# A one-token attention and feed-forward kernel: other load order, the feed-forward moved to the middle, and the output gathered in eight adjacent partitions

## The chip, the cores and the metric

The kernel runs on one core of one Trainium2 chip. A core has TensorE (PE, matrix products; its weight loads are shown as PEld), VectorE (DVE), ScalarE (ACT), GpSimd (POOL) and SyncE (SP), which run their own instruction lists and meet at semaphores, and 16 DMA engines that carry out the transfers which SP and ACT issue. The metric is the device time of one execution in microseconds (us); lower is better.

## The reference, cut to what matters

Two tokens (batch B = 2, one position each, D = 448) go through a layer norm; the result `xn` feeds an attention over the last W = 2048 positions of a given cache, and a small feed-forward net that gates it:

```
xn = layernorm(x)                                   # 2 x 448
q  = (xn @ wq)            -> 16 heads of 256        # wq 448 x 4096
k, v = caches[:, :, -2048:, :], 8 kv heads, each used by 2 query heads
p  = softmax(q . k / 16)                            # over 2048 positions
s  = (p @ v, all heads side by side) @ wo           # wo 4096 x 448
h  = relu(xn @ w1)                                  # w1 448 x 1792
g  = silu(h @ w2)                                   # w2 1792 x 448
out = x + s * g
```

All tensors are bfloat16. The arithmetic is tiny; the bytes are not. K and V are 4 x 4096 KB each, wq and wo 3584 KB each, w1 and w2 1568 KB each: 44.1 MB in all, each byte read once.

## The kernel before

**Units.** The work is cut into four units u = 0..3 (`NU`): batch u // 2, and four of the eight kv heads. The 128 partitions hold the 4 heads x 32 runs of positions; a partition holds 64 positions (`NT`) of one head. For a unit, `do_T` (16 calls, one for each chunk of four positions per partition) transposes K on PE into one of five PSUM banks `tb0`..`tb4`, and DVE or ACT evacuates it to `kt`; `do_S` multiplies four transposed chunks by the queries (`qz`) into the bank `sbk`; `softmax` finds the maximum (DVE, with two short PE steps to bring it across partitions), shifts, exponentiates on ACT, transposes the weights on PE and sums; `do_PV` multiplies them by V, in four quarters of eight products each; `attend_scale` divides by the sum (DVE) and `attend_turn` brings the result to the layout `at_exp`. `scores(u)` is all chunks of `do_T` with the `do_S` between them.

**Order.** Every engine's list is the order in which the Python code records its operations; there is no scheduler. On PE: the sixteen transposes of unit 0, the query projection `do_q` (L390), the scores and softmax of unit 0, then for u = 1, 2, 3 `scores(u)` and `softmax(u, values(u-1))`, where the PV products of the unit before fill the gaps in the softmax. After unit 3's softmax come, on PE, the feed-forward net (`do_H`, `do_hT`, `do_F`, L413 to L443), then `do_PV(3)`, its scale and turn, two products that spread `at_exp` into `at2` (one a batch, L500), and the output projection (L506 to L511).

**Column groups.** Products with few output rows are issued in fours with `tile_position=(0, 32*i)`: each writes its own 32 of the 128 PSUM partitions, so four run at once in four column groups of the array. The output projection has 32 steps j of four products with 112 columns each; the weights have two columns (the two batches). Its result therefore stands in partitions 0, 1, 32, 33, 64, 65, 96, 97. `do_F` is made in the same way with 14 steps.

**Loads.** SP issues all large loads, in the order in which they are recorded, and each waits for its buffer: K0, wq, K1 and V0 at once; K2 after the transposes of unit 0 (L202), V1 after the query product, K3 after the transposes of unit 1, V2 after PV of unit 0; w1 and w2 (into `kbuf0`, L478) after the transposes of unit 2; V3 in two parts after PV of unit 1; wo (into `kbuf1`, L488) in five parts of 12, 12, 4, 2 and 2 steps after the transposes of unit 3. wq lies in `vbuf1` until V1 takes its place.

**End.** DVE multiplies by the gate and adds x (L513, L515); SP and ACT each store one batch (L517), four partitions that lie 32 apart, and SP waits for both stores (L519).

## Time and profile before

| | us |
|---|---|
| median of 4 runs (112.70 to 112.95) | 112.85 |
| the profiled execution | 112.70 |
| its span, first to last instruction | 110.9 |
| outside the span | 1.8 |
| PE busy / weight loads | 74.9 (68%) / 50.1 (45%) |
| DVE busy | 48.1 (43%) |
| ACT busy | 35.3 (32%) |
| SP's DMA queue, share of 16 engines | 93.5%, 44.11 MB |

Times in the profile are counted from the start of the span. The profile has a page (busy times, the span in 40 slices, the queues, the chain that ended last, the costliest groups) and views that are asked for: the chain of waits in order of time, the timeline of a window (start, length, engine, line, operation, output <- inputs, count, and in brackets the idle time before it with what ended it), stretches with busy time and granted clock, and the durations at one source line. "128*4 128x512" in a row is 128 rows by 4 weight columns, and a moving operand of 128 partitions by 512.

### The profile page before, as it was taken

The numbers are of one execution on the slowest core, as the hardware profiler recorded it, in microseconds if no ns is written. First come the engines' busy times: TensorE is split into PE (matmuls) and PEld (weight loads), VectorE is DVE, ScalarE is ACT, GpSimd is POOL, SyncE is SP. The second block draws the span as 40 slices with busy tenths as digits, with TensorE's granted clock in tenths as the row PEclk, the third lists the DMA queues.
The fourth block names the chain that finished last, engine by engine and source line by source line (L and its number), as shares of the span: only waits on it lengthen the run. The fifth ranks groups of instructions, "written<-read, shape, count | busy, mean of one in ns | idle before, by whom it ended". The sixth has DMA issues, their size and how long they took to land.

```text
span 110.9 us, 1921 instructions
## 1 busy us (share of the span) xinstructions
PE 74.9 (68%) x845; PEld 50.1 (45%) x845; DVE 48.1 (43%) x110; ACT 35.3 (32%) x43; POOL 2.0 (2%) x11
## 2 busy tenths in 40 slices
PE   0010299995338999859999949699985667293480
PEld 0000299952027977413777513297632336022350
DVE  2182042953534256553776653477546231404001
ACT  1960036760020647602276602076820200000000
POOL 6000000000000000000000000000000000000000
PEclk9999999999995589995999995899999755555555
DMA  3988979898899899889989998998999998999920
GB/s 107 461 379 379 520 331 496 355 567 372 378 520 425 378 414 520 384 378 532 417 366 437 479 402 378 520 425 378 401 396 421 502 425 375 398 431 419 400 81 1
DMA packets 2619, 44.22 MB, mean 399 GB/s; under 512 B 306, under 2 KB 564, under 8 KB 948
## 3 DMA queue, kind: packets, MB, share of 16 engines
q1 hardware_dynamic: 2584, 44.11, 93.5%
q8 instruction: 6, 0.10, 0.4%
q10 hardware_dynamic: 28, 0.00, 0.0%
q14 instruction: 1, 0.01, 0.0%
HBM read 44.11 MB, written 0.00 MB: 398 GB/s over the span
## 4 chain that ended last, share of the span: by engine, by line
DMA 56%; PE 34%; DVE 4%; SPq 1%; issue 1%; ACT 1%
DMA kbuf<-in_A_k_cache_dram 34%; PE tb L285 25%; DMA kbuf<-in_A_wo_dram 22%; PE sbk L265 5%; PE obk L265 2%; SPq L36 1%; PE mbk L265 1%; DVE s_sb L335 1%; ACT e_sb L340 1%; DVE rm L318 1%; DVE q_n L399 1%; PE mbk L345 1%; DVE pt L350 0%; DVE qz L409 0%; PE mbk L403 0%
## 5 line engine op out<-in xcount | busy, mean ns | idle before, releaser
L285 PE MATMUL tb<-ident_f,kbuf 128*128 128x128 f32 x256 | 36.5, 306 | 6.4 <-DMA kbuf<-in_A_k_cache_dram 6.4
L285 PEld LDWEIGHTS tb<-ident_f,kbuf 128*128 128x128 f32 x256 | 33.4, 161 | 10.6 <-DMA kbuf<-in_A_k_cache_dram 6.6
L295 ACT ACTIVATE kt<-tb 128x1024 bf16<-128x1024 bf16 x28 | 27.4, 1023 | 26.2 <-PE tb L285 26.2
L293 DVE COPY kt<-tb 128x1024 bf16<-128x1024 bf16 x36 | 24.8, 691 | 21.7 <-PE tb L285 21.7
L265 PE MATMUL obk<-vbuf,pt 128*16 128x512 bf16 x128 | 13.7, 538 | 2.4 <-DMA vbuf<-in_A_v_cache_dram 2.4
L265 PE MATMUL sbk<-kt,qz 128*32 128x512 bf16 x128 | 11.0, 393 | 1.6 <-DVE kt L293 1.1
L340 ACT ACTIVATE e_sb<-s_sb 128x512 bf16<-128x512 f32 x4 | 2.5, 629 | 22.9 <-DVE s_sb L335 22.9
L265 PEld LDWEIGHTS obk<-vbuf,pt 128*16 128x16 bf16 x128 | 3.2, 101 | 7.1 <-DMA vbuf<-in_A_v_cache_dram 3.3
L265 PE MATMUL mbk<-ident,xg 2*128 2x2 bf16 x7 | 0.3, 163 | 7.4 <-DVE xg L237 7.4
L265 PEld LDWEIGHTS sbk<-kt,qz 128*32 128x32 bf16 x128 | 2.7, 94 | 5.4 <-DVE kt L293 2.1
L265 PE MATMUL obk<-kbuf,at 128*2 128x112 bf16 x128 | 3.7, 291 | 2.1 <-DMA kbuf<-in_A_wo_dram 1.8
L372 DVE TENSOR_SCALAR o_sb<-obk,rs 128x512 bf16<-128x512 f32 x4 | 2.9, 737 | 4.3 <-PE obk L265 4.3
L318 DVE TENSOR_REDUCE rm<-sbk 128x4 f32<-128x512 f32 x4 | 2.8, 692 | 4.3 <-PE sbk L265 4.3
L350 DVE COPY pt<-mbk 128x512 bf16<-128x512 bf16 x4 | 1.7, 425 | 5.6 <-PE mbk L345 5.6
L345 PE MATMUL mbk<-ident,e_sb 128*128 128x128 bf16 x16 | 2.2, 286 | 2.6 <-ACT e_sb L340 2.6
L265 PEld LDWEIGHTS obk<-kbuf,at 128*2 128x2 bf16 x128 | 2.6, 112 | 3.1 <-DMA kbuf<-in_A_wo_dram 2.6
L265 PEld LDWEIGHTS mbk<-ident,xg 2*128 2x128 bf16 x7 | 0.3, 100 | 7.4 <-DVE xg L237 7.4
L345 PEld LDWEIGHTS mbk<-ident,e_sb 128*128 128x128 bf16 x16 | 1.3, 122 | 5.0 <-ACT e_sb L340 5.0
L323 PE MATMUL mbk<-ident_f,rm 128*1 128x128 f32 x4 | 1.1, 270 | 3.4 <-DVE rm L321 3.4
L265 PE MATMUL mbk<-one_f,mall 1*128 1x1 f32 x8 | 1.6, 270 | 2.5 <-DVE mall L330 2.5
L335 DVE SCALAR_TENSOR_TENSOR s_sb<-sbk,bias,low 128x512 f32<-128x512 f32 x4 | 3.0, 751 | 0.1
L265 PEld LDWEIGHTS mbk<-ssum,gsum 128*128 128x128 f32 x8 | 1.6, 252 | 3.1 <-DVE pt L350 3.1
(68 smaller groups left out, 37.1 us busy)
## 6 DMA issues: line engine op xcount, KB each, us to landing
kbuf<-in_A_k_cache_dram SPq DMA_DIRECT2D x4, 4096.0 KB, 27.2
vbuf<-in_A_v_cache_dram SPq DMA_DIRECT2D x3, 4096.0 KB, 37.1
vbuf<-in_A_wq_dram SPq DMA_DIRECT2D x1, 3584.0 KB, 20.1
kbuf<-in_B_w_dram SPq DMA_DIRECT2D x2, 1568.0 KB, 23.8
vbuf<-in_A_v_cache_dram SPq DMA_DIRECT2D x1, 3072.0 KB, 25.9
kbuf<-in_A_wo_dram SPq DMA_DIRECT2D x2, 1344.0 KB, 22.2
vbuf<-in_A_v_cache_dram SPq DMA_DIRECT2D x1, 1024.0 KB, 27.8
kbuf<-in_A_wo_dram SPq DMA_DIRECT2D x1, 448.0 KB, 24.3
```

Of the source, the lines that this page charges most:

```text
L36: o = _Op(eng, lambda e: e.dma_start(dst, src), [d for d in deps if d is not None], True)
L265: return lambda e: e.matmul(out_ap, lhsT=lhsT, rhs=rhs, start=start, stop=stop, skip_group_check=True, **kw)
L285: o = pr.op(PE, lambda e, n=n, lo=lo: e.matmul(bank_f[:, n * 128:(n + 1) * 128], lhsT=src_f[:, lo:lo + 128], rhs=ident_f[:, :], start=True ...
L293: evac[n_th] = pr.op(DVE, lambda e: e.tensor_copy(dst[:, :], bank[:, :]), deps)
L295: evac[n_th] = pr.op(ACTE, lambda e: e.activation(dst[:, :], bank[:, :], ACT.Copy), deps)
L318: v = pr.op(DVE, lambda e: e.tensor_reduce(out=rm4[:, :], in_=view(sbk, 0, [[1, 4], [4, 128]]), axis=AX.X, op=ALU.max), [st["S", u]])
L335: v = st["shift", u] = pr.op(DVE, lambda e: e.scalar_tensor_tensor(out=view(s_sb, 0, [[4, 128], [1, 4]]), in0=view(sbk, 0, [[4, 128], [1, ...
L340: a = st["exp", u] = pr.op(ACTE, lambda e: e.activation(e_sb[:, :], s_sb[:, :], ACT.Exp, accum_out=ssum[:, 0:1]), [v, st.get(("Pt", u - 1) ...
L345: o = pr.op(PE, lambda e, j=j: e.matmul(mb16[:, 512 + 128 * j:640 + 128 * j], lhsT=e_sb[:, 128 * j:128 * j + 128], rhs=ident[:, :], start= ...
L350: v = st["pt", u] = pr.op(DVE, lambda e: e.tensor_copy(view(pt[u % 2], 0, [[256, 2], [16, 16], [8, 2], [1, 8]]), view(mb16, 512, [[256, 2] ...
L372: st["osb", u] = st["obk"] = pr.op(DVE, lambda e: e.tensor_scalar(out=o_sb[:, :], in0=obk[:, :], scalar1=rs[:, u:u + 1], scalar2=None, op0 ...
L399: v = st["obk"] = pr.op(DVE, lambda e: e.tensor_scalar(out=q_n[:, :], in0=obk[:, :], scalar1=SCALE, scalar2=None, op0=ALU.mult), [o])
```

## The change

1. **Load order.** SP first loads two of the seven slots of wq (8 KB a partition), then K0, then the other five slots; w1 and w2 are issued behind V0, without a wait, into a buffer of their own (`wf`), so that they come before K2. wo goes into `kbuf0`, which is free after the transposes of unit 2, in six parts of 8, 8, 6, 4, 4, 2 steps; the first 16 steps are the first head group, the other 16 the second.
2. **Feed-forward in the middle.** `do_H`, `do_hT` and `do_F` stand between unit 1's softmax and unit 2's scores on every engine, using the banks `tb0` and `tb1` there.
3. **Eight adjacent partitions.** The weights of `do_F` and of the output projection lie in zeroed buffers with gaps (`h_z`, `at_z`, `GAP` = 11 columns a step); a window of eight columns that starts at 3 - i puts the two batches in rows i and 4 + i. The four products of a step now accumulate into the same eight PSUM rows, without `tile_position`. The gate, the last two DVE operations and x have 8 partitions instead of 128 (or 8 scattered ones), and ACT stores the whole output in one transfer and waits for it.
4. **Spreading per unit.** `attend_turn` writes 128 columns, and a new `attend_spread(u)` (one product, one DVE copy) is done for each unit: for units 0 and 1 in the next-but-one unit's scores, for 2 within PV of unit 3, for 3 ahead of the output projection.
5. **Unit 3.** Its PV goes to another bank (`tb3`, which ACT zeroes after the last evacuation); PE gets products whose result nobody reads, `idle_work`: 3 before PV of unit 3, 3 after `attend_scale(3)`, 1 before the last spread.
6. **Small things.** `low` is laid out over 512 columns, so that the shift (L335) reads and writes plain rows; `qmask` has 8 columns; `fold16` is new; two more buffers are zeroed on POOL.

```diff
-    WO_PARTS = [12, 12, 4, 2, 2]
+    WO_PARTS = [8, 8, 6, 4, 4, 2]
+    NWO = 16
+    FIRST = 2
+    NROW = 4 * B
+    GAP = NROW + 3
...
-        wq_sb, w1_sb, w2_sb, wo_sb = vbuf[1], kbuf[0], kbuf[0], kbuf[1]
+        wq_sb, w1_sb, w2_sb, wo_sb = vbuf[1], wf, wf, kbuf[0]
-        wo_src = A_wo.rearrange("(p j) n -> p (j n)", j=32)
+        wo_src = A_wo.rearrange("(v p j) n -> v p (j n)", v=2, j=NWO)
...
+        d_wq = [pr.dma(SP, wq_sb[:, 0:FIRST * HC], wq_src[:, 0:FIRST * HC])]
         load_k(0)
-        d_wq = pr.dma(SP, wq_sb[:, 0:SLOTS * HC], wq_src)
+        d_wq.append(pr.dma(SP, wq_sb[:, FIRST * HC:SLOTS * HC], wq_src[:, FIRST * HC:SLOTS * HC]))
         load_k(1)
         load_v(0)
+        st["w1"] = pr.dma(SP, w1_sb[:, 0:W2_AT], w1_src)
+        st["w2"] = pr.dma(SP, w2_sb[:, W2_AT:W2_AT + 14 * D].rearrange("p (hf f) -> p hf f", hf=2), w2_src)
...
-                out=view(s_sb, 0, [[4, 128], [1, 4]]), in0=view(sbk, 0, [[4, 128], [1, 4]]), scalar=bias[:, 0:1],
-                in1=view(low, 0, [[0, 128], [1, 4]]), op0=ALU.add, op1=ALU.min),
+                out=s_sb[:, :], in0=sbk[:, :], scalar=bias[:, 0:1], in1=low[:, :], op0=ALU.add, op1=ALU.min),
...
+        def attend_spread(u):
+            b, v = divmod(u, 2)
+            o = st["m_at", u] = pr.op(PE, mm(mbk_ap(256, NWO), at_exp[:, :], fold16[:, :], True, True),
+                                      [st["at", u], v_fold16, st["mbk"]])
+            st["at_z", v] = st["mbk"] = pr.op(DVE, lambda e: e.tensor_copy(
+                view(at_z, NWO * GAP * v + 3 + 4 * b, [[GAP, NWO]]), mbk_ap(256, NWO)), [o, p_z])
...
-                    o = pr.op(PE, mm(view(fbk, 0, [[1, NCOL]], n=B, p0=32 * i), h_sb[:, 2 * f:2 * f + 2], w2_sb[:, lo:lo + NCOL],
-                                     f == 0, f == 13, tile_position=(0, 32 * i)), deps)
+                    o = pr.op(PE, mm(view(fbk, 0, [[1, NCOL]], n=NROW), h_z[:, f * GAP + 3 - i:f * GAP + 3 - i + NROW],
+                                     w2_sb[:, lo:lo + NCOL], f == 0 and i == 0, f == 13 and i == 3), deps)
...
+        def idle_work(n):
+            wbk = tb[2][:, :].bitcast(F32).tensor
+            deps = [evac[NU * NCHUNK - 2], v_fold]
+            for _ in range(n):
+                pr.op(PE, mm(view(wbk, 0, [[1, 512]]), ident[:, :], kt[0][:, 0:512], True, True), deps)
+                deps = []
...
         softmax(1, values(0))
         attend_scale(0)
+        do_H()
+        do_hT()
+        do_F()
         load_v(2)
         scores(2)
...
         load_v(3, (0, 48, 64))
+        d_wo, j0 = {}, 0
+        for n in WO_PARTS:
+            v, j = divmod(j0, NWO)
+            d_wo[j0] = pr.dma(SP, wo_sb[:, j0 * D:(j0 + n) * D], wo_src[v, :, j * D:(j + n) * D], [st["T", 2]])
+            j0 += n
         scores(3)
...
         softmax(3, values(2))
         attend_scale(2)
-        do_H()
-        attend_turn(2)
-        do_hT()
-        do_F()
-        do_PV(3)
+        idle_work(3)
+        do_PV(3, (0,))
+        attend_turn(2)
+        do_PV(3, (1,))
+        attend_spread(2)
+        do_PV(3, (2, 3))
         attend_scale(3)
+        idle_work(3)
         attend_turn(3)
...
+        idle_work(1)
+        attend_spread(3)
...
-                m_o = pr.op(PE, mm(obk[32 * i:32 * i + B, 0:NCOL], at2[:, 2 * j:2 * j + 2], wo_sb[:, lo:lo + NCOL],
-                                   j == 0, j == 31, tile_position=(0, 32 * i)), deps)
+                m_o = pr.op(PE, mm(obk[0:NROW, 0:NCOL], at_z[:, j * GAP + 3 - i:j * GAP + 3 - i + NROW],
+                                   wo_sb[:, lo:lo + NCOL], j == 0 and i == 0, j == 2 * NWO - 1 and i == 3), deps)
...
-        d_o = [pr.dma((SP, ACTE)[b], out[b, 0, :].rearrange("(i n) -> i n", i=4),
-                      view(out_sb, 0, [[1, NCOL]], n=4, p0=b, pstep=32), [v_o]) for b in range(B)]
-        pr.op(SP, None, d_o)
+        d_o = pr.dma(ACTE, out[:, 0, :].rearrange("b (i n) -> (b i) n", i=4), out_sb[:, :], [v_o])
+        pr.op(ACTE, None, [d_o])
```

## The prediction

> **What bounds the kernel now.** I read the queue shares and the slices of the page first, then the chain of waits, then the timeline of the stretches that the change touches, then the granted clock by stretch. The page:

> ```profile
> DMA  3988979898899899889989998998999998999920
> GB/s 107 461 379 379 520 331 496 355 567 372 378 520 425 378 414 520 384 378 532 417 366 437 479 402 378 520 425 378 401 396 421 502 425 375 398 431 419 400 81 1
> q1 hardware_dynamic: 2584, 44.11, 93.5%
> ```

> SP's queue is never empty from slice 2 on. The bytes set the end, in whatever order they come. The chain says the same: two long waits for transfers, and a short tail after the last one.

> ```profile
> 0.74 12.35 DMA kbuf<-in_A_k_cache_dram
> 13.13 10.10 PE tb L285 x64
> ...
> 46.25 25.41 DMA kbuf<-in_A_k_cache_dram
> 71.70 1.97 PE tb L285 x16
> ...
> 83.03 24.44 DMA kbuf<-in_A_wo_dram
> 107.52 0.39 PE obk L265 x8
> 107.92 0.28 DVE tmp L513
> 108.23 0.28 DVE out_sb L515
> ```

> K0 has landed at 13.09, K3 at 71.66, the last piece of wo at 107.47. From K3 to the end of wo 15.27 MB follow (V2, w1, w2, V3, wo) in 35.81 us: 0.426 MB/us, the rate I use. How much room PE has below that is in the timeline:

> ```profile
> 71.70 1.97 PE L285 MATMUL tb<-ident_f,kbuf 128*128 128x128 f32 x16 [1.06 <-DMA kbuf<-in_A_k_cache_dram]
> ...
> 92.46 1.47 PE L265 MATMUL tb<-kbuf,h_sb 128*2 128x112 bf16 x56 [0.39 <-DVE h_sb L432]
> ...
> 96.35 3.59 PE L265 MATMUL obk<-vbuf,pt 128*16 128x512 bf16 x32 [2.41 <-DMA vbuf<-in_A_v_cache_dram]
> ...
> 102.38 1.29 PE L265 MATMUL obk<-kbuf,at 128*2 128x112 bf16 x48 [0.29 <-DVE at L502]
> 105.30 2.02 PE L265 MATMUL obk<-kbuf,at 128*2 128x112 bf16 x72 [1.62 <-DMA kbuf<-in_A_wo_dram]
> ```

> PE waits 1.06 us for K3, 2.41 for V3, 1.62 for wo: little slack in a chain of work from 13 to 96 that is otherwise PE's own. Last, the clock:

> ```profile
> 46.41:49.82 3.41, 1.67 (x18) 0.51 (x16) 2.05 (x6) 0.00 (x0) 0.00 (x0) 1.00 1.05 447
> 49.82:53.24 3.42, 3.42 (x30) 1.15 (x30) 1.33 (x3) 0.72 (x2) 0.00 (x0) 0.50 1.07 460
> 53.64:63.10 9.46, 9.46 (x96) 7.46 (x95) 6.34 (x11) 6.79 (x7) 0.00 (x0) 1.00 1.03 441
> 101.02:104.43 3.41, 1.75 (x52) 1.24 (x50) 0.62 (x3) 0.00 (x0) 0.00 (x0) 0.50 0.98 408
> ```

> Columns: stretch, length, busy PE, PEld, DVE, ACT, POOL, then granted clock, DMA share, GB/s. A stretch half idle (1.67 busy) is followed by one at 0.50; a full one (3.42) by full clock. The output projection ran at 0.50 throughout.

> **The change, part by part.**

> *Loads.* Bytes are the same, so the last piece of wo still lands near 107.5; two more cuts add a little (I take +0.1; 0 to +0.3). Within the queue two things move. The 1.05 MB of wq ahead of K0 delay K0 by 1.05/0.426 = 2.46, to 15.55 (the same-sized last part of V3 follows its first part by 98.81 - 96.34 = 2.47 where PE waits for them). The 3.21 MB of w1 and w2 now precede K2, V1, K3 and V2: 7.5 us later each, K3 at 79.2 and K2 near 59.5 (two units of 4.19 MB before K3). V3 (98.8) and wo keep their places. SP issues seven loads at the start instead of four, 0.6 us each, ahead of use. It issues wo behind V3, which waits for PV of unit 1 (80 in my sum); V2 feeds the engines until 88.9. No gap, nothing.

> *PE until unit 1 is done.* K0 is what PE waits for, so +2.46 passes through T(0), q, unit 0's softmax, T(1), unit 1's softmax. V0 and K1 land where they did (41 and 33, estimates from the rate) and stay hidden. PE reaches 53.78 + 2.46 = 56.24. What T(0) gains or loses by when full clock comes is +-1.

> *Feed-forward in the middle.* Before, T(2) started at 53.64, while DVE still scaled unit 0 (53.90 for 0.73). Now `do_H` waits for that scale: 0.85. From H to the start of F took 89.56 to 92.46 = 2.90 at clock 0.50; its two PE pieces (1.48, 0.54) halve at full clock, so 1.9 to 2.9, I take 2.6. F: 56 products, before in fours, 1.47 us. Without column groups they run one after another. Price at 0.50: the projection's first 48 took 1.29 with one lasting 0.29, so 11 further groups take 1.00, 91 ns for one stream of 112 columns. At full clock: half, 46; the four 128-column transposes of q start (0.40 - 0.22)/3 = 60 ns apart, 52 for 112 columns. I take 50. F is 2.8 (full) to 5.1 (half), taken 3.4. Together 6.85 (5.6 to 8.9). T(2) starts near 63.0 against 53.64. K2 is there. Hidden before: H, F and the gate stood in PE's wait for V3, and DVE and ACT were idle.

> *Units 2 and 3.* T(2) and its softmax took 53.64 to 70.64. The gate chain (0.27 + 0.22 + 0.85 + 0.28 and three hops) now holds `tb1` and stands ahead of DVE's first evacuation: about +0.4; the spread +0.1. T(3) starts at 80.5; K3 (79.2) is no longer what it waits for. T(3) and softmax took 71.70 to 88.56 = 16.86, +0.1: 97.5. The plain `low` may take some hundredths off each shift (0.75); I take nothing.

> *PV of unit 3.* 32 products: 16 took 1.04 at full clock, so 1.9 to 3.4; idle work 0.65 to 1.3; turn 0.27, spread 0.21. 3.0 to 5.2, taken 3.6: 101.1, against 99.94. V3 (98.8) is hidden. Then scale 0.75, turn 0.27, mask 0.23, one spread 0.21 and copy 0.20, five hops: 1.95, where the second spread and copy (0.5) are saved. The three idle products lie under the scale at full clock (0.65 of 0.75) and stick out by 0.5 at half. The projection starts at 103.0 against 102.38.

> *Output projection.* 128 products in a row: 6.4 at full clock, 11.6 at half. Before: 32 groups x 91 = 2.9, mostly waiting for wo. The first 16 steps are in by 103.1 and the rest by 107.5, so from 103.0 on PE is the later one; I take 6.9 (some of it at half clock) and 0.2 for the last to come out: 110.1, against 107.87. [...]

> *End.* From the last product to the end of the span 3.04 now. One store for two: the completion records have ACT's at 110.15 and SP's at 110.51. I take -0.3 (0 to -0.6, both stores left at once). Two DVE operations of 112 columns keep their 0.28.

> **Sum.** 110.1 + 3.04 - 0.3 = 112.85 for the span, against 110.9: +1.95 on the profiled execution of 112.70. That one lies 0.15 below the median, so 112.85 + 1.95 = **114.8**.

> [...]

> **The rivals.**

> *The transfers still set the end (21 in 100).* Idle work keeps full clock and PE catches up, so that T(3) waits for K3. For it: K3 at 79.2 is only 1.3 before my PE. Then: 79.2 + 17.0 = 96.2; the last quarter of PV waits for V3 and ends at 99.5; the projection starts at 101.4, has done 16 steps at 104.6 and all at 108.1 with the last piece at 107.6. Span 108.1 + 3.04 - 0.3 = 110.85: -0.05, time 112.8. It turns faster by 0.23 us (0.2%, what a measurement of this kernel can tell from no change) only if the store saves its full 0.36 and the last piece isn't late. Against: each of the three PE terms must come out at its lower end.

> *Half clock in the tail (12 in 100).* A softmax gap halves the clock, as it did at 87, and the short waits for DVE after PV keep any stretch from being full. PV costs 1.6 more, the projection 1 to 4.7 more: 117.5 to 121. For it: clock 0.50 from 87 to the end now, with 2.56 of 3.42 busy. Against: six to nine us of unbroken products.

> *A gap in the queue (2 in 100).* If PV of unit 1 came after 88.9, V3 and wo would wait; PE would have to lose 9 us more. Each us then costs one.

> **How the numbers follow.** The forecast (113.3 to 116.8 for itself, from the bounds of F, of PV and of the store) has 65 in 100. Its low end already is slower than before by 0.4%. The transfer-bound rival splits into 12 within 0.2% and 9 faster. Slower: 65 + 12 + 2 = 79. The range 112.7 to 117.6 leaves out the deep half-clock end and the best store, about 15 in 100.

> **What would show it.** T(0) starts near 15.5; T(2) near 63 and T(3) near 80 with no wait for K; F's 56 products last about 3 us; wo pieces land before PE asks, so no row of the projection waits for DMA; its products start some 50 ns apart; one store. Wrong, if the projection waits for wo (rival one), if its products are 90 ns apart (rival two), or if four products without column groups start closer than 46 ns.

## The result, and the profile after

The changed kernel takes 114.65 us (median of 10 executions, 113.15 to 116.25) where the kernel before takes 112.93 (median of 15, 112.70 to 113.06): slower. The ratio is 1.0108, 95% interval 1.0078 to 1.0139; it is lower than that of the medians, 1.0152, because the comparison leaves out executions more than 1.5% above the fastest, and the changed kernel's own spread is wider than that (so are those of a_k0first, a_noidle and a_twostores below). The profiled execution is the slowest of them, 116.25, with a span of 114.2; a second profile of the same kernel, at 114.19 (span 112.4), stands beside it here.

From the page of the changed kernel: the slices of PE and of DMA, the queue of the large loads, and the chain's shares by engine.

```profile
PE   0010069996725999958669999857999965999992
...
DMA  3989899999899899999999999899899989999100
...
q1 hardware_dynamic: 2864, 44.11, 91.2%
...
PE 64%; DVE 16%; DMA 12%; issue 2%; ACT 2%; SPq 0%
```

Before, DMA held 56% of the chain and PE 34%; now PE holds 64% and DMA 12%. The DMA slices are empty at the end, while PE is at nine tenths until the last but one: the bytes are in, and PE is still at work. The chain of waits of the same execution, in order of time (start, length, what, how many):

```profile
59.29 4.29 PE tb L281 x56
64.13 0.85 DVE tmp L477
...
81.09 2.64 PE tb L301 x16
...
105.55 6.40 PE obk L281 x128
```

The last entry is the whole output projection without a gap. The timeline of PE has the starts, and a wait, where there is one, in brackets:

```profile
59.29 4.27 PE L281 MATMUL tb<-wf,h_z 128*8 128x112 bf16 x56 [0.45 <-DVE h_z L460]
...
80.95 2.78 PE L301 MATMUL tb<-ident_f,kbuf 128*128 128x128 f32 x16
...
100.29 1.03 PE L281 MATMUL tb<-vbuf,pt 128*16 128x512 bf16 x8
...
105.48 6.46 PE L281 MATMUL obk<-kbuf,at_z 128*8 128x112 bf16 x128
```

These are the feed-forward's 56 products, the first transposes of unit 3, the first PV products of unit 3, and the projection: none waits for a transfer any more. The last piece of wo landed at 107.47, as before, and the last product ended at 111.94. The second profile of the changed kernel, the same rows:

```profile
57.41 4.34 PE L281 MATMUL tb<-wf,h_z 128*8 128x112 bf16 x56 [0.45 <-DVE h_z L460]
...
79.06 2.85 PE L301 MATMUL tb<-ident_f,kbuf 128*128 128x128 f32 x16
...
98.45 1.03 PE L281 MATMUL tb<-vbuf,pt 128*16 128x512 bf16 x8
...
103.69 6.46 PE L281 MATMUL obk<-kbuf,at_z 128*8 128x112 bf16 x128
```

Everything from unit 2 on stands 1.8 to 1.9 us earlier, with nearly the same lengths, and the projection ends at 110.15. This execution is the nearer to the median, so I set the prediction's steps against it.

Where the time went, from the profile before (span 110.9) to this one (112.4): the projection starts 1.31 later (102.38 to 103.69) and takes 0.97 longer from its first product to its last (5.49 to 6.46), and what follows the last product is 0.80 shorter (3.04 to 2.24). 1.31 + 0.97 - 0.80 = 1.48.

### The profile page after: what moved, and what is told of

Its sections match the earlier page's. It is cut to its first block, busy times and chain, and to the rows that moved or that the text cites. A ratio compares the mean times of both kernels' runs of the same rounds, so it can differ in the third digit from the quotient of the medians.

```text
span 114.2 us, 1945 instructions
## 1 busy us (share of the span) xinstructions
PE 82.0 (72%) x853; PEld 57.4 (50%) x854; DVE 49.4 (43%) x114; ACT 36.0 (32%) x44; POOL 2.3 (2%) x12
## 3 DMA queue, kind: packets, MB, share of 16 engines
q1 hardware_dynamic: 2864, 44.11, 91.2%
HBM read 44.11 MB, written 0.00 MB: 386 GB/s over the span
## 4 chain that ended last, share of the span: by engine, by line
PE 64%; DVE 16%; DMA 12%; issue 2%; ACT 2%; SPq 0%
PE tb L301 29%; DMA kbuf<-in_A_k_cache_dram 12%; PE obk L281 12%; PE tb L281 8%; PE sbk L281 8%; PE mbk L281 4%; DVE kt L309 3%; DVE rm L334 2%; PE mbk L360 2%; DVE s_sb L351 2%; ACT e_sb L355 2%; DVE o_sb L392 1%; DVE mrow L342 1%; PE mbk L339 1%; DVE mall L346 1%
## 5 line engine op out<-in xcount | busy, mean ns | idle before, releaser
L301 PE MATMUL tb<-ident_f,kbuf 128*128 128x128 f32 x256 | 37.5, 310 | 8.5 <-DMA kbuf<-in_A_k_cache_dram 8.5
L301 PEld LDWEIGHTS tb<-ident_f,kbuf 128*128 128x128 f32 x256 | 34.2, 164 | 12.8 <-DMA kbuf<-in_A_k_cache_dram 8.6
L281 PE MATMUL obk<-vbuf,pt 128*16 128x512 bf16 x96 | 9.4, 473 | 0.0
L281 PE MATMUL obk<-kbuf,at_z 128*8 128x112 bf16 x128 | 6.5, 213 | 0.0
L281 PEld LDWEIGHTS obk<-kbuf,at_z 128*8 128x8 bf16 x128 | 6.3, 87 | 0.0
L281 PE MATMUL tb<-wf,h_z 128*8 128x112 bf16 x56 | 4.3, 259 | 0.4 <-DVE h_z L460 0.4
L281 PEld LDWEIGHTS tb<-wf,h_z 128*8 128x8 bf16 x56 | 4.1, 110 | 0.5 <-issue 0.5
L281 PEld LDWEIGHTS obk<-vbuf,pt 128*16 128x16 bf16 x96 | 2.2, 92 | 2.5 <-issue 1.2
## 6 DMA issues: line engine op xcount, KB each, us to landing
vbuf<-in_A_v_cache_dram SPq DMA_DIRECT2D x1, 3072.0 KB, 15.5
```

Of the source, the lines that this page charges most:

```text
L281: return lambda e: e.matmul(out_ap, lhsT=lhsT, rhs=rhs, start=start, stop=stop, skip_group_check=True, **kw)
L301: o = pr.op(PE, lambda e, n=n, lo=lo: e.matmul(bank_f[:, n * 128:(n + 1) * 128], lhsT=src_f[:, lo:lo + 128], rhs=ident_f[:, :], start=True ...
```

## The experiments

"Row" means products that accumulate one after another into the same eight PSUM rows, as the change has them; "groups" means the four column groups of before. Each run was compared with runs of the kernel before on the same chip (medians 112.87 to 112.90); ratios have 95% intervals. In the diffs the first column says what is taken from, or added to, the kernel named.

| run | kernel | median us (range, n) | ratio to before |
|---|---|---|---|
| a_groups | changed, groups again | 112.66 (112.49 to 112.97, 10) | 0.9984 (0.9975 to 0.9994) |
| a_ffn_end | changed, feed-forward at the end again | 112.37 (112.26 to 113.55, 10) | 0.9973 (0.9950 to 0.9996) |
| b_ffnmid | before, feed-forward in the middle | 112.87 (112.70 to 113.30, 10) | 1.0003 (0.9993 to 1.0013) |
| a_k0first | changed, K0 first again | 113.62 (112.68 to 114.67, 10) | 1.0024 (0.9993 to 1.0055) |
| b_wqfirst | before, two slots of wq first | 112.53 (112.46 to 112.60, 5) | 0.9967 (0.9954 to 0.9980) |
| mix | a_ffn_end, K0 first, more idle work | 112.93 (112.52 to 113.66, 10) | 1.0004 (0.9983 to 1.0026) |
| a_noidle | changed, without idle work | 114.23 (112.61 to 116.17, 10) | 1.0079 (1.0045 to 1.0113) |
| a_twostores | changed, two stores | 114.67 (113.01 to 115.92, 10) | 1.0088 (1.0056 to 1.0120) |
| after_again | the changed kernel | 114.44 (114.19 to 114.75, 4) | 1.0151 (1.0133 to 1.0169) |
| best | a_ffn_end, K0 first, wo in seven parts | 112.72 (112.56 to 113.03, 11) | 0.9988 (0.9978 to 0.9997) |
| best2 | a_ffn_end, wo in eight parts, less idle work | 112.33 (112.26 to 112.46, 5) | 0.9956 (0.9943 to 0.9970) |
| best2_noidle | best2 without idle work | 112.37 (112.20 to 113.82, 12) | 0.9975 (0.9949 to 1.0001) |

### Column groups back into the changed kernel (a_groups)

```diff
-  mm(obk[0:NROW, 0:NCOL], at_z[:, j * GAP + 3 - i:j * GAP + 3 - i + NROW], wo_sb[:, lo:lo + NCOL], ...)
+  mm(obk[32 * i:32 * i + NROW, 0:NCOL], at_z[:, j * GAP + 3:j * GAP + 3 + NROW], wo_sb[:, lo:lo + NCOL],
+     ..., tile_position=(0, 32 * i))
...
-  d_o = pr.dma(ACTE, out..., out_sb[:, :], [v_o])
+  d_o = [pr.dma((SP, ACTE)[b], out[b]..., view(out_sb, 0, [[1, NCOL]], n=4, p0=4 * b, pstep=32), [v_o])
+         for b in range(B)]
```

The same edit is made in `do_F`, and the gate, the last two DVE operations and x stand in 128 partitions again; load order, place of the feed-forward and idle work stay as changed.

> The changed kernel with column groups again in F and in the output projection (and so two stores of scattered partitions), load order, feed-forward in the middle and idle work kept. Theory: F takes 1.3 to 1.5 us in place of 4.3, T(3) waits for K3 (79.1), the projection takes 2.9 us of PE and is paced by wo (107.5), the two stores cost 0.75 more than one: 112.9 (112.6 to 113.4). Rival two (the wq slots ahead of K0 and the extra work make PE late by themselves): PE stays late, the projection does not wait for wo, 113.8 or more.

Measured: 112.66, 0.9984 of before; the whole loss is gone, although the feed-forward is still in the middle. Timeline of PE:

```profile
57.57 1.48 PE L283 MATMUL tb<-wf,h_z 128*8 128x112 bf16 x56 [0.45 <-DVE h_z L462]
...
79.21 3.67 PE L303 MATMUL tb<-ident_f,kbuf 128*128 128x128 f32 x16 [0.72 <-DMA kbuf<-in_A_k_cache_dram]
...
103.68 1.57 PE L283 MATMUL obk<-kbuf,at_z 128*8 128x112 bf16 x88
105.92 0.37 PE L283 MATMUL obk<-kbuf,at_z 128*8 128x112 bf16 x16 [0.66 <-DMA kbuf<-in_A_wo_dram]
...
107.57 0.27 PE L283 MATMUL obk<-kbuf,at_z 128*8 128x112 bf16 x8 [0.17 <-DMA kbuf<-in_A_wo_dram]
```

The projection starts at 103.68, to 0.01 us where the changed kernel's second profile has it. So a late start is not enough for a loss: 88 products are done in 1.57 us, then PE waits for wo again, and the end is 0.3 us after the last piece (107.53 landed, 107.84 ended). From the same start the changed kernel's products end at 110.15: in this pair the whole difference up to there is the projection's. No run has groups in only one of the two products. What follows the last product is back at 3.02 us. The feed-forward's 56 products took 1.48 at clock 0.50, where the row took 4.3 with most of it at 0.50: 26 ns against 76 a product, so for four column groups this pair of rows shows 2.9 times the throughput, at clocks that differ. With half clock in nearly all of it, the row took 5.24 (best2_noidle, below), 3.5 times the 1.48. The single records agree: in the projection of the kernel before, at clock 0.50, four products start within 10 ns of each other and the next four 93 ns later; in F of the changed kernel (116.25) the products start one by one, 93 ns apart at 0.50 and 49 from 62.2 on, at full clock.

### The feed-forward back at the end (a_ffn_end)

```diff
-  wq_sb, w1_sb, w2_sb, wo_sb = vbuf[1], wf, wf, kbuf[0]
+  wq_sb, w1_sb, w2_sb, wo_sb = vbuf[1], kbuf[0], kbuf[0], kbuf[1]
...
-  do_H(); do_hT(); do_F()          # between unit 1's softmax and scores(2)
...
   scores(2)
+  st["w1"] = pr.dma(SP, ..., [st["T", 2]]); st["w2"] = pr.dma(SP, ..., [st["T", 2]])
...
   attend_scale(2); idle_work(3)
+  do_H(); attend_turn(2); do_hT(); attend_spread(2); do_F(); idle_work(3)
+  do_PV(3, (0, 1, 2)); do_PV(3, (3,))
```

wo is loaded after the transposes of unit 3, as before; the row of products, the single store and wq ahead of K0 stay.

> The changed kernel with the feed-forward net, its loads and wo's place as before the change (after unit 3's softmax), keeping two slots of wq first, the eight adjacent partitions, one store and idle work. Theory: PE is 2.46 late at T(2), reaches T(3) near 73 (K3 lands at 71.7), ends unit 3's softmax near 90, and the net fills PE's wait for V3; the projection starts between 102 and 104.5: 113.2 (112.4 to 114.8), better than the changed kernel. Rival one (only the projection without column groups costs): 114.65.

Measured: 112.37, 0.9973: the loss is gone here too, and with the row of products still in place. Timeline of PE:

```profile
96.24 1.47 PE L278 MATMUL tb<-vbuf,pt 128*16 128x512 bf16 x24 [0.34 <-DMA vbuf<-in_A_v_cache_dram]
...
100.94 1.74 PE L278 MATMUL obk<-kbuf,at_z 128*8 128x112 bf16 x32
103.09 5.23 PE L278 MATMUL obk<-kbuf,at_z 128*8 128x112 bf16 x96 [0.41 <-DMA kbuf<-in_A_wo_dram]
```

The time lies just below my range, and PE was less late than I took it: T(2) starts at 54.65, 1.0 later than before instead of 2.46, and T(3) at 71.70, as before. The feed-forward in a row takes 2.91 at full clock in the time in which PE would wait for V3. The projection starts at 100.94, so its 6.46 of work fit ahead of the last piece (107.48) but for the end: it stops at 108.32.

### The feed-forward in the middle of the kernel before (b_ffnmid)

```diff
   load_v(0)
+  st["w1"] = pr.dma(SP, w1_sb..., w1_src); st["w2"] = pr.dma(SP, w2_sb..., w2_src)   # into their own buffer
...
   attend_scale(0)
+  do_H(); do_hT(); do_F()
```

K0 is first, the products are in groups, both stores and the late part of the kernel are as before.

> The kernel before the change with the feed-forward net (column groups kept) between unit 1's softmax and unit 2's scores, w1 and w2 loaded ahead of K2 into their own buffer, all else as before. Theory: T(2) starts near 59 to 60 (net about 5 us, K2 near 59.5), T(3) waits for K3 at 79.2, its softmax ends near 96.2, PV of unit 3 ends between 99.5 and 101, the projection is still paced by wo: 112.9 (112.7 to 113.6). Rival five (the move costs by itself, since it leaves PE's wait for V3 empty): 114 or more.

Measured: 112.87, 1.0003 (0.9993 to 1.0013): no change. Timeline of PE:

```profile
60.04 3.67 PE L288 MATMUL tb<-ident_f,kbuf 128*128 128x128 f32 x16 [3.95 <-DMA kbuf<-in_A_k_cache_dram]
...
79.51 1.97 PE L288 MATMUL tb<-ident_f,kbuf 128*128 128x128 f32 x16 [1.03 <-DMA kbuf<-in_A_k_cache_dram]
...
103.64 0.76 PE L268 MATMUL obk<-kbuf,at 128*2 128x112 bf16 x48 [0.29 <-DVE at L502]
...
107.73 0.36 PE L268 MATMUL obk<-kbuf,at 128*2 128x112 bf16 x8 [0.20 <-DMA kbuf<-in_A_wo_dram]
```

K2 and K3 are late here by the 3.21 MB of w1 and w2, and PE waits 3.95 and 1.03 for them; the projection starts 1.26 later than before and still ends 0.4 after the last piece of wo. With the two runs above this closes the square (medians; which load is first differs too, and is named):

| | groups | row |
|---|---|---|
| feed-forward at the end | 112.93 (before, K0 first), 112.53 (wq first) | 112.37, best2 112.33 (both wq first); best 112.72, mix 112.93 (both K0 first) |
| feed-forward in the middle | 112.87 (K0 first), 112.66 (wq first) | **114.65** (wq first), 113.62 (K0 first) |

Neither half costs anything alone. Moving the feed-forward uses up the slack ahead of the projection, and the row needs just that slack: 6.46 us of products between the start and the last piece of wo. Only where both are in is the kernel with wq first the longer one, by 1.0 (114.65 against 113.62); in the other three cells it is the shorter one (the kernels of a cell differ in more than that).

### K0 first in the changed kernel (a_k0first)

```diff
-  d_wq = [pr.dma(SP, wq_sb[:, 0:FIRST * HC], wq_src[:, 0:FIRST * HC])]
   load_k(0)
-  d_wq.append(pr.dma(SP, wq_sb[:, FIRST * HC:SLOTS * HC], wq_src[:, FIRST * HC:SLOTS * HC]))
+  d_wq = [pr.dma(SP, wq_sb[:, 0:SLOTS * HC], wq_src)]
```

> The changed kernel with K0 loaded first again (all of wq behind it), all else kept. Theory (PE is late all the way, so what starts it later counts): K0 lands 2.3 to 2.5 us earlier, T(3) no longer starts on PE's own time (80.95 in the profile of the changed kernel) but when K3 lands (79.1), so 1.1 to 1.8 us come off: 113.2 (112.6 to 114.0), against 114.65. Rival one (only the end costs: the projection without column groups, whatever stands ahead of it): no change, 114.65 +-0.3. In both the projection's 128 products take 6.4 to 7 us.

Measured: 113.62, with executions from 112.68 to 114.67. Timeline of PE:

```profile
79.56 3.67 PE L300 MATMUL tb<-ident_f,kbuf 128*128 128x128 f32 x16 [0.67 <-DMA kbuf<-in_A_k_cache_dram]
...
103.13 6.46 PE L280 MATMUL obk<-kbuf,at_z 128*8 128x112 bf16 x128
```

T(0) starts at 13.32 instead of 15.49, but T(2) at 61.28 against 61.68 in the second profile of the changed kernel: in these two executions 0.4 of the lead is left by then. At T(3) PE waits for K3, which w1 and w2 have made late and which lands at 79.52 here (78.99 there), so T(3) starts 0.50 later than in the second profile. That the projection is still 0.56 earlier comes from the clock, which is 1.00 from 83.86 on: idle work and PV take 3.43 instead of 4.85. So this pair of profiles does not show what the earlier start is worth. The times do: the medians differ by 1.0 (114.65 - 113.62), and though the ranges overlap, the intervals of the two ratios (0.9993 to 1.0055 and 1.0078 to 1.0139) don't. About 1.0 of the 1.7 us is therefore K0's late start, and rival one, no change, is out.

### Only two slots of wq first, in the kernel before (b_wqfirst)

```diff
-  load_k(0)
-  d_wq = pr.dma(SP, wq_sb[:, 0:SLOTS * HC], wq_src)
+  d_wq = [pr.dma(SP, wq_sb[:, 0:2 * HC], wq_src[:, 0:2 * HC])]
+  load_k(0)
+  d_wq.append(pr.dma(SP, wq_sb[:, 2 * HC:SLOTS * HC], wq_src[:, 2 * HC:SLOTS * HC]))
```

> The kernel before the change with one thing altered: two slots of wq ahead of K0. Theory: T(0) starts 2.3 to 2.5 us later, the wait for K3 (1.06) goes, T(3) starts 1.4 us later, and the rest is taken from the wait for V3 (2.41): 112.9 (112.7 to 113.1), no change. Rival four (the delay of the first transfer passes to the end as it is): 115.3.

Measured: 112.53, 0.9967 (0.9954 to 0.9980): faster, where I expected no change. K0 lands 2.2 later, T(3) starts at 72.71 instead of 71.70, and PE still waits 1.50 for V3, so the delay is absorbed as I thought. The gain is at the start of the stream. SP's first issue and the stretch from 1 to 2 us (last two columns: share of the DMA engines, GB/s), first of the kernel before:

```profile
0.74 0.65 SPq L36 DMA_DIRECT2D kbuf<-in_A_k_cache_dram  x1
...
1.00:2.00 1.00, 0.00 (x0) 0.00 (x0) 0.00 (x0) 0.00 (x0) 0.57 (x3) 1.00 0.01 2
```

and of b_wqfirst:

```profile
0.74 0.38 SPq L36 DMA_DIRECT2D vbuf<-in_A_wq_dram  x1
...
1.00:2.00 1.00, 0.00 (x0) 0.00 (x0) 0.00 (x0) 0.00 (x0) 0.57 (x4) 1.00 0.66 100
```

The issue of 8 KB a partition takes 0.38 where that of K0's 32 KB a partition takes 0.65, and data flow earlier: the first packets of the large queue start at 1.74 instead of 2.17. The last piece of wo lands at 107.22 instead of 107.47, and the time is 0.37 less. Of the 0.43 us at the start, 0.25 is left at the last landing. That the issue's length is the reason is argued: no run loads something else of 8 KB a partition first. But the changed kernel, with wq first too, has its first packet at 1.74 and 92 GB/s from 1 to 2 us, and a_k0first, with K0 first, has 2 GB/s there.

### K0 first and more idle work, with the feed-forward at the end (mix)

a_ffn_end with the diff of a_k0first, six idle products instead of three ahead of PV of unit 3, and two before its last quarter.

> Load order and place of the feed-forward net as before the change; eight adjacent partitions, products in a row, one store, spread per unit, wo in six parts by head group; idle work 3 after unit 3's softmax, 6 before PV of unit 3, 2 before its last quarter, 3 and 1 in the tail. Theory: T(3) starts at 71.7 as before, the net hides in the wait for V3, the projection starts near 101.4 and ends with the last piece of wo near 108.1, and the one store ends 2.25 after the last product in place of 3.04: 112.3 (111.9 to 113.0), faster than both if the clock is full in the tail. If the clock is half there, the projection takes 9 to 11.6: 113.5 to 116. Rival one (a projection without column groups costs by itself): 113.5 or more even at full clock.

Measured: 112.93 (112.52 to 113.66), 1.0004. It is worse than a_ffn_end by 0.56. Its profile is of an execution of 113.16, and there PE is late. It waits 2.95 us for K3, the clock is 0.50 from 71.63 to 75.05, and the first sixteen transposes of unit 3 take 3.54 instead of 1.95 (in a_ffn_end, with full clock). And the idle products (five of the six are in the trace) are now work on the path:

```profile
97.33 1.24 PE L277 MATMUL tb<-kt,ident 128*128 128x512 bf16 x5 [0.16 <-issue]
98.50 1.47 PE L277 MATMUL tb<-vbuf,pt 128*16 128x512 bf16 x24
```

V3's first part landed at 96.47, and PV starts at 98.50, after the idle work and an F that ended late (97.16, against 95.14 in a_ffn_end); the projection starts at 102.66 instead of 100.94. It ends at 109.12, so that the last piece of wo, which lands at 107.82 instead of 107.48, costs nothing in this execution.

### Without idle work (a_noidle)

```diff
-        idle_work(3)
         do_PV(3, (0,))
...
         attend_scale(3)
-        idle_work(3)
...
-        idle_work(1)
```

> The changed kernel without its seven idle products, all else kept. Theory: PE is late there and nearly unbroken without them, so the three ahead of PV of unit 3 only stand in its way (1.06 to 1.3 us at half clock, 0.65 at full) and those under the scale cost up to 0.5; the clock comes back by itself: 114.0 (113.2 to 114.8), against 114.65. Rival three (the idle products are what brings the full clock back): the projection's products start 91 ns apart for 3 us or more, 116 to 119.

Measured: 114.23 (112.61 to 116.17): 0.4 below the changed kernel's median, inside a spread of 3.6. Timeline of PE:

```profile
98.42 1.03 PE L281 MATMUL tb<-vbuf,pt 128*16 128x512 bf16 x8 [1.00 <-DVE o_sb L392]
...
103.78 6.46 PE L281 MATMUL obk<-kbuf,at_z 128*8 128x112 bf16 x128
```

Where the three products stood, PE waits 1.00 for DVE, and the PV products start within 0.03 of the second profile's. PV runs at half clock in both, and the projection at full clock in both, so rival three is out: the full clock comes back without idle products. In the changed kernel the idle work neither costs nor brings anything that these runs could show.

### Two stores, each of four adjacent partitions (a_twostores)

```diff
-  d_o = pr.dma(ACTE, out..., out_sb[:, :], [v_o]); pr.op(ACTE, None, [d_o])
+  d_o = [pr.dma((SP, ACTE)[b], out[b]..., out_sb[4 * b:4 * b + 4, :], [v_o]) for b in range(B)]
+  pr.op(SP, None, d_o)
```

> The changed kernel with the output stored by two transfers of four adjacent partitions, one issued by SP and one by ACT, and SP waiting for both, as before the change. Theory: from the end of the last product to the end of the span it takes 3.0 in place of 2.25; time 115.4 (114.5 to 116). If the wait at the end is the same for one store and for two: 2.25 and 114.65.

Measured: 114.67, and 2.37 us from the last product to the end of the span, against 2.24 with one store and 3.04 before: not the 3.0 that I expected, but nearly the rival's figure. The issues, of the kernel before and then of a_twostores:

```profile
108.53 0.66 SPq L36 DMA_DIRECT2D out_dram<-out_sb  x1
108.54 0.56 ACTq L36 DMA_DIRECT2D out_dram<-out_sb  x1
```

```profile
109.84 0.34 SPq L36 DMA_DIRECT2D out_dram<-out_sb  x1
109.85 0.27 ACTq L36 DMA_DIRECT2D out_dram<-out_sb  x1
```

The issue of four partitions that lie 32 apart takes about twice as long, and they land 1.98 (SP) and 1.61 (ACT) us after their issue starts, where the later of the adjacent ones lands 1.35 after. So of the 0.8 us by which the end is shorter, about 0.1 is the second store and most of the rest the scatter; a_groups, the changed kernel with two scattered stores, has 3.02 as well.

### The changed kernel again (after_again)

> The changed kernel once more, for a second profile. Theory: its executions differ by where half-clock stretches of 3.4 us fall on PE's work, since PE sets its end: K0 (15.3), K3 (79.1) and the last piece of wo (107.5) land where they did within 0.2 us, while T(3) starts anywhere from 79.1 to 81.5 and the projection anywhere from 101.5 to 105.5, and its end is that start + 6.4 + 2.25. Median 114.65 again (114.2 to 115.1). If the transfers were what differs, the landings would move with the end.

Measured: 114.44 (114.19 to 114.75). The profile is the one shown above. What makes it 1.8 us shorter than the first is the granted clock, at three places. The 64 transposes of T(0) take 9.13 instead of 10.04 (full clock is on record from 19.50, against 21.24), which by the start of q is 0.8 us. The start of T(1) gives 0.5 (half clock until 39.98, against 41.72). The rest, 0.6, comes in the second softmax. PV products of unit 0 in the second softmax, first profile and then second profile of the changed kernel:

```profile
52.36 1.88 PE L281 MATMUL obk<-vbuf,pt 128*16 128x512 bf16 x16
```

```profile
50.92 1.04 PE L281 MATMUL obk<-vbuf,pt 128*16 128x512 bf16 x16
```

The clock was 0.50 from 51.96 to 55.4 in the first, 1.00 at that place in the second. The landings are the same in both (last piece of wo 107.47 and 107.39). The second profile's last stretches (length, busy PE, PEld, DVE, ACT, POOL, granted clock, DMA share, GB/s):

```profile
94.59:98.00 3.41, 2.62 (x16) 1.16 (x17) 1.17 (x3) 0.49 (x2) 0.00 (x0) 0.50 0.99 414
98.00:101.42 3.42, 3.42 (x31) 0.76 (x33) 0.59 (x3) 0.00 (x0) 0.00 (x0) 0.50 1.01 417
101.42:104.83 3.41, 3.15 (x45) 1.73 (x38) 1.27 (x3) 0.00 (x0) 0.00 (x0) 1.00 1.00 403
```

PV falls into half clock, the projection into full clock.

### Towards a version that beats both (best, best2, best2_noidle)

best is a_ffn_end with K0 first, wo in parts 8, 4, 4, 6, 4, 4, 2, two idle products ahead of PV, and none ahead of its last quarter.

> K0 first and the feed-forward net at the end, as before the change; eight adjacent partitions, products in a row, one store; wo in parts of 8, 4, 4, 6, 4, 4, 2; idle products 3 ahead of the net, 2 ahead of PV of unit 3, 3 and 1 in the tail. Theory: T(3) starts at 71.7, PV of unit 3 ends when V3 has landed (99.3), the projection starts near 100.9 at full clock, does not wait for wo's second part and ends 0.4 after the last piece, 107.9 to 108.3, the span 2.25 later: 112.1 (111.9 to 112.5), faster than the kernel before. Rival one (products in a row cost by themselves): 113 or more.

Measured: 112.72, 0.9988, above my range. The last piece of wo lands at 107.86; the projection starts at 101.23, waits 0.63 for the piece of six steps at 105.17, and ends at 108.68, 0.8 after the last piece. b_wqfirst had shown what K0 first costs, so wq goes first again:

```diff
-    WO_PARTS = [8, 8, 6, 4, 4, 2]
+    WO_PARTS = [8, 4, 4, 4, 4, 4, 2, 2]
...
         attend_scale(2)
-        idle_work(3)
         do_H()
...
         do_F()
-        idle_work(3)
         do_PV(3, (0, 1, 2))
```

This is best2, as a diff against a_ffn_end.

> Two slots of wq first (its first packets start 0.4 us earlier than K0's did, 1.74 against 2.17), the feed-forward net at the end as before the change, eight adjacent partitions with products in a row, one store; wo in parts of 8, 4, 4, 4, 4, 4, 2, 2; idle products only 3 and 1 in the tail. Theory: T(3) starts near 72, PV of unit 3 ends when V3 has landed, near 99.3, the projection starts near 101, follows the pieces of wo and ends 0.5 after the last one, 107.8 to 108.0, the span 2.25 later: 112.0 (111.8 to 112.5), faster than the kernel before and than the one with only the wq slots moved (112.53). If the net's products in a row make PV late: 112.6 to 113.5.

Measured: 112.33, 0.9956 (0.9943 to 0.9970): faster than the kernel before by 0.54 us and than the changed kernel by 2.3. Timeline of PE:

```profile
71.42 1.96 PE L298 MATMUL tb<-ident_f,kbuf 128*128 128x128 f32 x16 [0.75 <-DMA kbuf<-in_A_k_cache_dram]
...
96.21 1.47 PE L278 MATMUL tb<-vbuf,pt 128*16 128x512 bf16 x24 [0.70 <-DMA vbuf<-in_A_v_cache_dram]
...
100.92 4.32 PE L278 MATMUL obk<-kbuf,at_z 128*8 128x112 bf16 x80
105.43 2.84 PE L278 MATMUL obk<-kbuf,at_z 128*8 128x112 bf16 x48 [0.18 <-DMA kbuf<-in_A_wo_dram]
```

The waits for K3, V3 and wo are back. The row ends 0.64 after the last piece (108.27 against 107.63), 0.24 more than the groups did before (0.40), and the adjacent store gives back 0.80: a gain of 0.56 at the end. The last piece lands 0.16 later than before, which leaves the 0.4 between the two spans (110.9 and 110.5); the medians are 0.54 apart.

best2_noidle leaves out the last four idle products (3 and 1 ahead of the projection).

> The same without any idle product. Theory: F and PV keep PE busy enough before; the wait for V3's last part and for the scale leaves a stretch half idle, so the projection may run at half clock (91 ns a product) until it has filled a stretch: 112.0 if the clock stays full, 113 to 115 if it falls. The idle products are worth the difference between the two kernels.

Measured: 112.37 (112.20 to 113.82, 12 executions); four of the twelve are above 112.5, three of them above 113, where the five of best2 end at 112.46. The medians are the same. With so few executions of best2, whether the four products keep the long ones out stays open. The one profile of best2_noidle has F at half clock (91 ns a product, F ends at 97.60) and still starts the projection at 100.95, at full clock.

## Why the prediction was right, and where its steps were off

The direction, the mechanism and the size held: 114.8 predicted, 114.65 measured. The steps, with two executions of the changed kernel (us; "taken" is the prediction's value):

| step | taken | at 116.25 | at 114.19 |
|---|---|---|---|
| T(0) starts | 15.6 | 15.38 | 15.49 |
| unit 1's softmax done | 56.24 | 55.96 | 54.08 |
| feed-forward detour, end of unit 1's softmax to T(2)'s start | 6.85 | 7.54 | 7.60 |
| of it F | 3.4 | 4.21 | 4.27 |
| T(2) start to T(3) start | 17.5 | 17.45 | 17.38 |
| T(3) starts | 80.5 | 80.95 | 79.06 |
| T(3) and softmax of unit 3 | 17.0 | 18.11 | 18.16 |
| idle work and PV | 3.6 | 4.79 | 4.85 |
| end of PV to projection | 1.95 | 1.63 | 1.62 |
| projection starts | 103.0 | 105.48 | 103.69 |
| projection | 6.9 + 0.2 | 6.46 | 6.46 |
| last product to the end | 2.74 | 2.24 | 2.24 |
| span | 112.85 | 114.2 | 112.4 |

**Loads.** K0's delay of 2.46 came out as 2.25 to 2.36. K3 at 79.2 was right: PE waits for it until 79.2 to 79.6 in a_groups, b_ffnmid and a_k0first. The last piece of wo, taken 0.1 later, landed at 107.4 to 107.5, unchanged, but as a sum of two effects that I had not priced: wq first starts the stream earlier (-0.25 in b_wqfirst), and order and cuts of the other loads cost something (107.82 to 107.86 in the kernels with the new cuts and K0 first, 107.63 in best2 with eight parts). Taken apart: the order of the loads alone gives 107.69 (b_ffnmid, K0 first), the new cuts of wo (with the new order of its rows) alone 107.82 with K0 first (mix, against 107.47) and 107.48 with wq first (a_ffn_end, against 107.22), and both together, with K0 first, 107.85 (a_k0first). So the cuts cost 0.26 to 0.35, where I took 0.1; each figure is one execution's.

**F.** The 3.4 was too low, inside the bounds of 2.8 to 5.1: 4.2 to 4.3, because most of F ran at half clock (76 ns a product as the mean; the bounds of 50 and 91 both nearly appeared, in the first profile's F itself: 93 apart at 0.50, until 62.2, and 49 after).

**T(3).** I had PE late there, by 1.3 against K3. In the slowest execution it is late by 1.8; in the usual one PE reaches T(3) at 79.06, just after K3 has landed (78.99), since T(0), T(1) and unit 1's softmax had more of the full clock. My +-1 on that term was too narrow: 55.96 and 54.08 are both the same kernel.

**Unit 3.** This is the term that failed outright. From T(3)'s start to the end of PV I took 20.6 and measured 22.9 and 23.0, more than 17.0 and the upper bound of 5.2 together (22.2). PV and the idle work were at half clock, which I had priced and not taken: 4.8, inside the bounds. The upper bound itself was low, for I took 3.4 for 32 products at half clock where the timeline before has 3.59. T(3) and its softmax, for which I gave no bounds, took 1.1 to 1.2 more than 17.0; most of that is the first transposes of unit 3, at half clock (2.85 for sixteen instead of 1.97), which I had not priced. It was made good by an early T(3) (-1.4), a faster path from PV to the projection (-0.3), and the projection at full clock (6.46 in place of 6.9 + 0.2, -0.6). That 110.1 was forecast for the end of the projection and 110.15 measured is thus partly cancellation, which is luck.

**The projection** was what I said: products 49 to 50 ns apart, no row that waits for wo, and PE later than the transfers. The part at half clock that the 6.9 contains is shown by no run: the row took 6.46, at full clock, in both profiles and in a_k0first and a_noidle. That a row alone is not the cause, and that it takes the moved feed-forward with it, is what I had not seen. I had priced the chain as one piece; a_ffn_end and a_groups show that either half alone is free. I also let K0's delay of 2.46 pass on to the end; against a_k0first it is worth about 1.0 in the medians, and in the profile of that kernel PE waits 0.67 for K3.

**End.** I took -0.3 for one store in place of two. It is -0.8, and the reason was wrong: two adjacent stores have nearly all of it. The plain `low` changed nothing, as taken: the shift is 0.75 in both kernels.

**The rivals.** That the transfers still set the end (112.8) was not seen: the changed kernel's lowest time is 113.15. With K0 first (a_k0first, lowest 112.68) some executions come down to it, and without idle work one does (a_noidle, 112.61). Half clock in the tail did happen, at PV, but not in the projection, which is where it would have been dear. No gap in the queue appeared. Idle work, which rival one counts on for the full clock, was not what brought it: PV was at 0.50 in spite of the three products ahead of it, and the full clock came from 101.42 with them and from 101.62 without (a_noidle). The stretch ahead of half clock that I showed had PE busy for 1.67 of its 3.41 us, so a stretch that costs the clock need not be an idle one (see the last section).

**The spread.** I gave no reason why a kernel with an even time should become uneven (113.15 to 116.25, before 112.70 to 113.06). The profiles show one: in the kernel before PE waits for landings, which don't move, so a half-clock stretch is absorbed; in the changed kernel PE's chain is the end, so each one is paid. The mean granted clock on record for each execution fits: 0.923 at 113.15 and 113.59, 0.909 or 0.910 at 114.22 to 115.25, 0.895 at 116.25; only 115.34, with 0.880, is out of order. That those without a profile differ for the same reason is still argued, not shown.

## What to carry to other kernels

Slack is shared: before two edits are priced alone, find whether they spend the same wait. Here a feed-forward moved forward and a projection with 6.5 us of products instead of about 3 were each free, because a wait for bytes covered either; together they cost 0.7 us, and 1.7 with wq ahead of K0, which starts PE later and by itself is a gain of 0.4. Keep cheap work in the waits at the end of a byte-bound kernel, start the stream with a load that is quick to issue if PE has slack for it (0.37 us in b_wqfirst), and store from adjacent partitions (from the last product to the end 3.04 us before, 2.37 in a_twostores).
